# Products with x over 64-row slices, two at a time in the two row halves of TensorE

## The chip, the cores and the metric

The kernel runs on one core of one Trainium2 chip. A core has five engines with queues of their own: TensorE (PE in the profile, with its weight loads in a row of their own, PEld), VectorE (DVE), ScalarE (ACT), GpSimd (POOL) and SyncE (SP), which here only issues DMAs. The metric is the device time of one execution in microseconds. The kernel before takes 1052.12 us, the median of 3 runs (1051.35 to 1052.48). Durations below come from one profiled execution of it, which took 1051.69 us.

## The reference

A gated sum of two branches over the same x, with 2048 tokens of width 448: attention with 16 heads of 28 columns, and a GeGLU feed-forward with 1792 hidden columns. All in fp32.

```python
g = _sigmoid((x * gate_w).sum(-1, keepdims=True))
# a: attention
qkv = (x @ wqkv).reshape(B, S, 3, H, Dh).transpose(2, 0, 3, 1, 4)
q, k, v = qkv[0], qkv[1], qkv[2]
scores = jnp.einsum("bhqd,bhkd->bhqk", q, k) * (Dh ** -0.5)
p = _softmax(scores, axis=-1)
o = jnp.einsum("bhqk,bhkd->bhqd", p, v)
a = o.transpose(0, 2, 1, 3).reshape(B, S, D) @ wo
# b: feed-forward
b = (_gelu(x @ w_gate) * (x @ w_up)) @ w_down
return g * a + (1 - g) * b
```

## The kernel before

**Precision.** An fp32 value is split into a high part, rounded to the type fp32r that TensorE streams fast, and a low part, the rest. A product of two split matrices is three products: high with high, high with low, low with high. ScalarE makes the high parts (`activation(..., Copy)`), VectorE or GpSimd the low ones (`tensor_tensor(..., subtract)`).

**Contracting with x.** x has 448 columns, that is three slices of 128 rows and one of 64. `PAIRS` (L42) lists the products of one output tile: 3 x 3 for the three whole slices, and 2 for the last: there the 64 high rows and the 64 low rows of x stand in one slice of 128 rows, multiplied once with the high and once with the low weights (stored twice, one copy for each half). So 11 products of 128 rows make one tile of 128 columns of weights by 512 tokens. `X` (L65) keeps x for the whole run as 7 slices of 128 partitions by 2048 tokens.

**Stage 1, q and k** (L84 to L193): 28 tiles `pqk` of 11 products each (`qk_tile`, L152), 7 column tiles for each of 4 token blocks. The raw inputs come in on SP and ACT queues, 8 ahead, and `SPLITS` says after which tile each is split: before the first tile stand the first weights and four slices of x. Each tile is split into high and low again and stored to DRAM (`qkd`).

**Stage 2, v and the gate** (`v_tile`, L172): 16 tiles `pv` of 128 tokens by 450 columns, 11 products each. Between them two small groups of products (`pb`, `pr`) bound the scores, so that softmax needs no maximum over rows. A branch (`tc.If`, L251) skips the exact row maxima, as here always. Every engine loads the flag and branches for itself.

**Stage 3, attention** (L285 to L408). For a head, `Q` and `K` hold four copies of 28 rows (high and low in the combinations that the split needs) and two rows for the bound, 114 rows in all, so one product of 128 keys by 512 queries gives finished scores. Heads are loaded one ahead, on the SP queue, into two pairs of buffers. A step is one key tile `kt` and half of the queries: two products into one of three score tiles `sc` (two PSUM banks each), then one `exp` by ScalarE over 128x1024 into `pt` (L307). The products with V (`values`, L310; fp32, four column tiles of 32 side by side into `po`) are done for four key tiles together, three steps after the last of them (`ENDS`, `LATE`): this gives a cycle of 8 steps, and 64 cycles in the run. Products of `x @ w_up` (`pu`, and of the first three tiles of `x @ w_gate`) fill between the steps, two per step (`RATE`), from a generator `up()` through `fill()`; after a finished tile one step goes without, while VectorE copies the one PSUM bank out (`u`, then to DRAM in `ud`).

**Stage 4, feed-forward and output** (L411 to the end). For each pair of hidden tiles: `hidden()` makes 11 products `pg` with w_gate for one token block, GELU on ScalarE, the product with the stored `u`, and the split `hl`; `down()` multiplies with w_down (`pd`, 128x448, 3 products per hidden tile) and adds into `acc` on VectorE. `down` of one block stands behind `hidden` of the next (`pend`). The attention output is multiplied with wo in `project()` in between. The last round writes `y` and sends it out.

**What sets the order.** Products are pinned in program order on TensorE (`mm`, L51, whose second line L52 every product has in the profile). Most of the DMAs, splits and copies are placed by a scheduler when the program is built; each engine then runs its list in order.

Of the kernel before, what the change touches and what calls it, by code (L numbers as in the profile page):

```python
# [17 lines left out]
P = 128  # L18
TB = 512
# [5 lines left out]
FC = 2  # L25
ENDS = (3, 7, 11, 15)
LATE = 3
RATE = 2
NB = 3
ORDER = (2, 3, 1, 4, 0, 5, 6)  # L30
AHEAD = 8
WARM = 9
LAG = 6
NR = 4 * DH + 2
# [3 lines left out]


# [6 lines left out]
def gated_mix(ctx: ExitStack, tc: tile.TileContext, xT, wqk, wvg, wg, wu, wd, wo, sel, ident, out):  # L46
# [13 lines left out]
    ud = dram.tile([NF + NB, P, S], F32, name="ud")  # L60
# [4 lines left out]
    X = keep.tile([P, 7, S], F32R, name="X")  # L65
    fw = ctx.enter_context(tc.tile_pool(name="fw", bufs=2))
    attn = ctx.enter_context(ExitStack())
    vp = attn.enter_context(tc.tile_pool(name="vp", bufs=1))
    V = vp.tile([P, NKT, H, 32], F32, name="V")
    nc.gpsimd.memset(V[:, :, :, DH:], 1.0)  # L70


    halves = {}

    def load_half(src, f, key, hi, mark=lambda ins: ins):
        raw = fw.tile([P, 4, P], F32, name="hraw")
        w = fw.tile([P, 8, P], F32R, name="half", bufs=3)
        mark(nc.sync.dma_start(out=raw, in_=src[f]))
        mark(hi(w[:, 0:4], raw))
        mark(nc.vector.tensor_tensor(w[:, 4:8], raw, w[:, 0:4].bitcast(F32), OP.subtract))  # L80
        halves[key, f] = w


    with ExitStack() as ph:  # L84
        wq = ph.enter_context(tc.tile_pool(name="wq", bufs=1))
        st = ph.enter_context(tc.tile_pool(name="st", bufs=1))
        wp = ph.enter_context(tc.tile_pool(name="wp", bufs=1))
        ps = ph.enter_context(tc.tile_pool(name="ps1", bufs=3, space=PSUM))
        psv = ph.enter_context(tc.tile_pool(name="psv", bufs=2, space=PSUM))
        psb = ph.enter_context(tc.tile_pool(name="psb", bufs=1, space=PSUM))  # L90

        WQK = wq.tile([P, NQK, 8, P], F32R, name="WQK")
        zero = st.tile([P, TB], F32R, name="zero")
        raws = [st.tile([P, TB], F32, name=f"raw{i}") for i in range(AHEAD)]
        WV = wp.tile([P, 8, VW], F32R, name="WV")
        selt = wp.tile([P, NQK, H], F32, name="selt")
        mx = wp.tile([P, NQK, NTB], F32, name="mx")
# [3 lines left out]
        warm = psb.tile([P, TB], F32, name="warm")  # L101
# [5 lines left out]
        SPLITS = {-1: ["w0", "x00", "x01", "x02", "x03"], 0: ["w1", "w2"], 1: ["w3", "x10"],  # L107
# [5 lines left out]

        def load():
            nonlocal issued
            if issued < len(loads):
                a = loads[issued]
                r = raws[issued % AHEAD]
                if a[0] == "w":
# [71 lines left out]
        while stored:  # L191
            store()
# [371 lines left out]
```

## Time and profile before

| | us |
|---|---|
| median of 3 runs | 1052.12 |
| the profiled execution | 1051.69 |
| its span (first to last instruction) | 1049.9 |
| stage 1, to the first `pv` | 77.4 |
| stage 2, to the branch | 37.8 |
| branch to the first scores | 3.9 |
| stage 3, to the last group of `po` | 637.9 |
| that group and the last `pu`, to the first `pg` | 6.2 |
| stage 4 | 286.8 |

A group of instructions stands in one line as `line engine op out<-in rows*columns shape xcount | busy us, mean ns of one | idle before, and what ended it`. A timeline line gives the start, the length from the first to the last of a merged run, the engine and the instructions. A matmul's length is modelled and longer than the distance to the next one, since they are pipelined; so the distance is worked out from runs: (length of the run - mean of one) / (count - 1). Times are us from the start of the span.

### The profile page before, as it was taken

How to read it: one execution, taken by the hardware profiler on the slowest of the kernel's cores; microseconds unless marked ns; L12 is line 12 of the kernel's file. 1: busy time of each engine (PE TensorE's matmuls, PEld its weight loads, DVE VectorE, ACT ScalarE, POOL GpSimd, SP SyncE). 2: the span in 40 equal slices, each digit the busy share in tenths (PEclk: the TensorE clock that was granted, in tenths of full speed). 3: DMA queues.
4: the chain of work that ended last, by engine and by line, in shares of the span. 5: the costliest groups of instructions: out<-in, count | busy, mean ns of one | idle time of the engine just before them, and what ended most of it. 6: DMA issues, size and time to landing. Idle time of an engine off the chain costs nothing.

```text
span 1049.9 us, 14556 instructions
## 1 busy us (share of the span) xinstructions
PE 1041.3 (99%) x5673; PEld 731.4 (70%) x5673; DVE 315.7 (30%) x512; ACT 610.5 (58%) x732; POOL 51.3 (5%) x38
## 2 busy tenths in 40 slices
PE   9999999999999999999999999999999999999998
PEld 6889765655655656656556556556588898899887
DVE  4552112111111011011011111110157666577555
ACT  5332477877777778778777777787643332233321
POOL 4322000000000000000000000000001011100000
PEclk9999999999999999999999999999999999999999
DMA  7865333332332332332332332331264323242223
GB/s 250 306 253 122 79 94 87 118 104 80 108 95 77 111 95 75 108 101 74 104 105 75 98 110 74 96 109 37 70 190 141 112 80 100 88 150 68 67 86 117
DMA packets 58906, 115.84 MB, mean 110 GB/s; under 512 B 12784, under 2 KB 18160, under 8 KB 55216
## 3 DMA queue, kind: packets, MB, share of 16 engines
q1 hardware_dynamic: 58544, 114.32, 36.2%
q8 instruction: 47, 0.77, 0.3%
q10 hardware_dynamic: 288, 0.52, 0.2%
q14 instruction: 27, 0.22, 0.1%
HBM read 74.44 MB, written 40.37 MB: 109 GB/s over the span
## 4 chain that ended last, share of the span: by engine, by line
PE 88%; ACT 0%; issue 0%; DVE 0%; ACTq 0%
PE sc L52 23%; PE po L52 22%; PE pd L52 16%; PE pu L52 16%; PE pg L52 11%; ACT pt L307 0%; DVE y L470 0%; ACT w L431 0%; ACTq L307 0%
## 5 line engine op out<-in xcount | busy, mean ns | idle before, releaser
L307 ACT ACTIVATE pt<-sc 128x1024 f32<-128x1024 f32 x512 | 477.9, 1040 | 160.7 <-PE sc L52 160.4
L52 PE MATMUL sc<-Q,K 128*128 128x512 f32 x1024 | 313.5, 398 | 1.7 <-issue 1.6
L52 PEld LDWEIGHTS sc<-Q,K 128*128 128x128 f32 x1024 | 187.1, 188 | 91.0 <-issue 54.8
L52 PE MATMUL pu<-X,half 128*128 128x512 f32 x748 | 233.3, 391 | 0.1
L52 PE MATMUL po<-pt,V 128*32 128x512 f32 x2048 | 233.0, 595 | 0.0
L352 DVE COPY u<-pu 128x512 f32<-128x512 f32 x68 | 47.0, 691 | 488.3 <-PE pu L52 477.4
L52 PEld LDWEIGHTS pu<-X,half 128*128 128x128 f32 x748 | 140.1, 188 | 32.4 <-issue 1.4
L52 PEld LDWEIGHTS po<-pt,V 128*32 128x32 f32 x2048 | 60.0, 109 | 138.2 <-issue 132.7
L52 PE MATMUL pd<-w,hl 128*128 128x448 f32 x672 | 140.1, 365 | 0.0
L52 PEld LDWEIGHTS pd<-w,hl 128*128 128x128 f32 x672 | 126.2, 188 | 11.1
L52 PE MATMUL pg<-X,half 128*128 128x512 f32 x484 | 114.0, 390 | 0.0
L52 PEld LDWEIGHTS pg<-X,half 128*128 128x128 f32 x484 | 90.9, 188 | 18.4
L52 PE MATMUL pqk<-X,WQK 128*128 128x512 f32 x308 | 70.9, 391 | 1.0 <-ACT X L143 0.8
L52 PEld LDWEIGHTS pqk<-X,WQK 128*128 128x128 f32 x308 | 57.5, 188 | 14.7 <-ACT X L143 1.5
L447 ACT ACTIVATE g<-pg 128x512 f32<-128x512 f32 x44 | 26.2, 594 | 70.3 <-PE pg L52 70.2
L448 DVE TENSOR_TENSOR g<-g,u 128x512 f32<-128x512 f32 x56 | 46.4, 837 | 50.8 <-ACT g L447 50.7
L449 ACT ACTIVATE hl<-g 128x512 fp32r<-128x512 f32 x56 | 35.2, 631 | 42.2 <-DVE g L448 36.8
L467 DVE SCALAR_TENSOR_TENSOR acc<-pd,gate,acc 128x448 f32<-128x448 f32 x80 | 52.7, 679 | 6.0 <-PE pd L52 5.9
L495 POOL TENSOR_TENSOR ohl<-oraw,ohl 128x1536 fp32r<-128x1536 f32 x4 | 14.0, 3502 | 704.8 <-ACT ohl L491 704.8
L450 DVE TENSOR_TENSOR hl<-g,hl 128x512 fp32r<-128x512 f32 x56 | 38.3, 687 | 10.6 <-ACT hl L449 8.5
L162 ACT ACTIVATE hl<-pqk 128x512 fp32r<-128x512 f32 x28 | 16.7, 598 | 41.6 <-PE pqk L52 39.7
L52 PE MATMUL pv<-WV,X 128*128 128x450 f32 x176 | 36.5, 367 | 0.0
(62 smaller groups left out, 357.0 us busy)
## 6 DMA issues: line engine op xcount, KB each, us to landing
ud<-u SPq DMA_DIRECT2D x68, 256.0 KB
qkd<-hl SPq DMA_DIRECT2D x28, 512.0 KB
K<-qkd SPq DMA_DIRECT2D x64, 224.0 KB
Q<-qkd SPq DMA_DIRECT2D x64, 224.0 KB
u<-ud SPq DMA_DIRECT2D x56, 256.0 KB
rb<-rdend SPq DMA_DIRECT2D x64, 64.0 KB
raw<-in_xT SPq DMA_DIRECT2D x14, 256.0 KB
hraw<-in_wu SPq DMA_DIRECT2D x14, 256.0 KB
```

The source lines that it names most:

```text
L52: return pin(nc.tensor.matmul(o, lhsT, rhs, start=start, stop=stop))
L162: pin(nc.scalar.activation(hl[:, 0], p, AF.Copy))
L307: nc.scalar.activation(pt, sc, AF.Exp, scale=SCALE)
L352: nc.vector.tensor_copy(u, p)
L447: nc.scalar.activation(g, pg, AF.Gelu_apprx_tanh)
L448: nc.vector.tensor_tensor(g, g, u, OP.mult)
L449: nc.scalar.activation(hl[:, 0], g, AF.Copy)
L450: nc.vector.tensor_tensor(hl[:, 1], g, hl[:, 0].bitcast(F32), OP.subtract)
L467: nc.vector.scalar_tensor_tensor(acc[:, t], p, g1, acc[:, t], OP.mult, OP.add)
L495: nc.gpsimd.tensor_tensor(O[:, 4:7], o[:, 0:3], O[:, 0:3].bitcast(F32), OP.subtract)
```

## The change

All products that contract over x use slices of 64 rows: 448 is 7 x 64, with no rest. `X` becomes 14 slices (7 high, 7 low): partitions 0 to 63 hold the tokens of the first half (blocks 0 and 1), partitions 64 to 127 those of the second (2 and 3). Weights are stored twice, once in each half of the partitions (`both`). A tile needs 21 products of 64 rows (`UNITS`). They are written alternately for a tile in the lower and one in the upper row half:

```diff
+NS = 7
+HALF = S // 2
-RATE = 2
-NB = 3
+RATE = 4
+NOUT = 68
+UNITS = [(NS * a + s, NS * b + s) for s in range(NS) for a, b in ((0, 0), (0, 1), (1, 0))]
-    X = keep.tile([P, 7, S], F32R, name="X")
+    X = keep.tile([P, 2 * NS, HALF], F32R, name="X")
-        def qk_tile(n):
-            tb, t = divmod(n, NQK)
-            for i, (x, w) in enumerate(pairs):
-                mm(p, WQK[:, t, w, :], X[:, x, s], i == 0, i == len(pairs) - 1)
+        def qk_pair(n):
+            b, t = divmod(n, NQK)
+            p = [ps.tile([P, TB], F32, name="pq") for _ in range(2)]
+            for i, (x, w) in enumerate(UNITS):
+                for g in range(2):
+                    mm(p[g], WQK[side(g), t, w], X[side(g), x, s], i == 0, i == len(UNITS) - 1)
```

`v_pair` does the same for two token tiles of stage 2, and `hidden(f, b)` for the blocks b and b + 2 in stage 4. In stage 1 each load becomes two DMAs of 64 partitions, and nine splits instead of five stand ahead of the first products:

```diff
-        SPLITS = {-1: ["w0", "x00", "x01", "x02", "x03"], 0: ["w1", "w2"], 1: ["w3", "x10"],
+        SPLITS = {-1: ["a0", "x00", "x01", "x02", "x03", "b0", "x04", "x05", "x06"],
+                  **{n: [f"a{n + 1}", f"b{n + 1}", f"x1{n}"] for n in range(6)}, 6: ["x16"],
-            sub = nc.vector if a in loads[:6] else nc.gpsimd
+            sub = nc.vector if done < len(SPLITS[-1]) else nc.gpsimd
```

Scores: `K` holds high and low (56 rows, then rows of ones) in each row half, `Q` has two layers, high and low, each twice in each row half, so 512 queries of scores are two products of 64 rows into one bank. Q takes 8 DMAs per head instead of 4, K 4 as before, and the bound 2 instead of 1. In a step the four products of the scores stand in one row half and up to four products of one `x @ w_up` tile in the other; `run` deals them out alternately. Two steps of a cycle get no units: the one with the values, and the one behind it.

```diff
+        def run(todo):
+            while todo[0] or todo[1]:
+                g = min((g for g in range(2) if todo[g]), key=lambda g: free[g])
+                todo[g].pop(0)()
+                free[g] = max(free[g], free[1 - g] - 1) + 1
-        def scores(h, kt, half):
+        def scores(h, kt, half, n):
+            n = min(n, left())
+            if n:
+                f = block["g"]
+                todo[f] += [unit] * n
+                to = (1 - f, 1 - f if n > 1 else f)
+            else:
+                f = min(range(2), key=lambda g: free[g])
+                to = f, 1 - f
             for c in range(2):
-                mm(sc[:, c * 512:(c + 1) * 512], K[:, kt * P:(kt + 1) * P],
-                   Q[:, half * 1024 + c * 512:half * 1024 + (c + 1) * 512], True, True)
+                g = to[c]
+                for a in range(2):
+                    todo[g].append(lambda g=g, a=a, c=c: mm(
+                        sc[:, c * 512:(c + 1) * 512], K[side(g), kt * P:(kt + 1) * P],
+                        Q[side(g), a, half * 1024 + c * 512:half * 1024 + (c + 1) * 512], a == 0, a == 1))
+            run(todo)
-        fill(11)
+        two_blocks()
-                    spaced(h, kt, half)
                     count += 1
+                    spaced(h, kt, half, 0 if due and count == LATE or count == LATE + 1 and h + kt > 3 else RATE)
```

`two_blocks` computes two tiles side by side in a score tile's two banks; one call stands ahead of the first scores, one ahead of the last values. In stage 4 the four `hidden` calls of a pair of hidden tiles now stand together ahead of its four `down` calls; the pool `gp` of w_down's split tiles is made only there (before, it was set aside ahead of attention); the output tile takes the two buffers of `gs` where `y` had three:

```diff
-                    y = tp.tile([P, TB], F32, name="y")[:, 0:D]
+                    y = tp.tile([P, TB], F32, name="gs", bufs=2)[:, 0:D]
+            for b in range(2):
+                for i, f in enumerate(chunk):
+                    if b == 0 and n * FC + i + 1 < NF:
+                        load_f(ORDER[n * FC + i + 1])
+                    for tb, hl in zip((b, b + 2), hidden(f, b)):
+                        hls.setdefault(tb, []).append(hl)
+            for i, tb in enumerate((0, 2, 1, 3)):
+                down(n, tb, hls[tb])
```

Three places of the built order follow. On PE, one cycle of attention in the middle of the run, from one group of values to the next. Before (sc are scores, pu products of `x @ w_up`, po values; the middle repeats):

```order
L52 MATMUL po<-pt,V 32x512 x16
L52 MATMUL sc<-Q_956,K_957 128x512 x2
L52 MATMUL pu<-X,half 128x512 x2
...
L52 MATMUL pu<-X,half 128x512
L52 MATMUL sc<-Q_956,K_957 128x512 x4
L52 MATMUL po<-pt,V 32x512 x16
```

That is 16 sc and 11 pu in a cycle. After, each product a half of the rows:

```order
L60 MATMUL po<-pt,V 32x512 x16
L60 MATMUL sc<-Q_1441,K_1442 128x512 x4
L60 MATMUL pu<-X,half 128x512
L60 MATMUL sc<-Q_1441,K_1442 128x512
...
L60 MATMUL pu<-X,half 128x512
L60 MATMUL sc<-Q_1441,K_1442 128x512 x8
L60 MATMUL po<-pt,V 32x512 x16
```

Now 32 sc and 21 pu stand in a cycle, pu and sc in turn for the most part, with 4 sc alone behind the values and 8 nearly alone ahead of them.

On PE, around the branch (gsc products stand in the branch that is not taken). Before:

```order
L250 TENSOR_LOAD flag
L52 MATMUL pu<-X,half 128x512 x2
L251 COMPARE_AND_BRANCH
...
L251 UNCONDITIONAL_BRANCH x2
L52 MATMUL pu<-X,half 128x512 x9
L52 MATMUL sc<-Q_956,K_957 128x512 x4
```

After:

```order
L60 MATMUL pq<-WV,X 128x450 x84
L294 TENSOR_LOAD flag
L295 COMPARE_AND_BRANCH
...
L295 UNCONDITIONAL_BRANCH x2
L60 MATMUL sc<-X,half 128x512 x42
L60 MATMUL pu<-X,half 128x512
```

The 11 pu around the branch needed only their own PSUM bank. The 42 products of `two_blocks` that now stand first write banks 0 and 1, which the last `v_pair` used, so their first waits for ScalarE's and VectorE's copies of those. On POOL the fills of Q's and K's constant rows, which stood ahead of the branch, now stand behind it but for one, and so do 11 of head 0's 12 loads on SP.

On ACT, the start of stage 4. Before:

```order
L447 ACT_TABLE_LOAD
L447 ACTIVATE g<-pg 128x512 x2
L449 ACTIVATE hl_8061<-g 128x512
L449 ACTIVATE hl_8091<-g 128x512
L447 ACTIVATE g<-pg 128x512
```

After:

```order
L553 ACTIVATE g<-gs 128x512 x2
L327 ACTIVATE half<-hraw 128x896
L555 ACTIVATE hl_10382<-g 128x512
L555 ACTIVATE hl_10388<-g 128x512
L527 ACTIVATE w<-draw 128x448 x2
L553 ACTIVATE g<-pg 128x512 x2
L553 ACTIVATE g<-gs 128x512
L527 ACTIVATE w<-draw 128x448
L555 ACTIVATE hl_10447<-g 128x512
```

The first GELUs of products (`g<-pg`) and the split of their result (`hl_10447`) now stand behind three splits of w_down (`w<-draw`), whose loads share one buffer `draw`; before, w_down's first tiles were loaded and split during attention.

More of the change, by code (lines that the diff above doesn't have):

```diff
@@ L358, in gated_mix, with unit, two_blocks, spaced @@
+        def unit():
+            nonlocal hold
+            product(block)
+            if block["n"] == len(UNITS):
+                hold = 3
+        def two_blocks():
+            sc = psc.tile([P, 1024], F32, name="sc")
+            todo = []
+            for g in range(2):
+                start(sc[:, g * 512:(g + 1) * 512])
+                b = dict(block)
+                todo.append([lambda b=b: product(b)] * len(UNITS))
+            block["n"] = len(UNITS)
+            run(todo)
         hold = 0
-        def fill(n):
+        def spaced(h, kt, half, n):
@@ L405, in gated_mix @@
         hold = 0
[L406 to L407 removed]
+        while left():
+            unit()
+            hold = 0
     attn.close()
```

367 lines of the change are left out of this document (199 added, 168 removed), and 3 rows, old and new, of the table SPLITS.

## The prediction

> **What bounds the kernel now.** I read the page's busy times first, then its chain, then the stages.
>
> ```profile
> span 1049.9 us, 14556 instructions
> PE 1041.3 (99%) x5673; PEld 731.4 (70%) x5673; DVE 315.7 (30%) x512; ACT 610.5 (58%) x732; POOL 51.3 (5%) x38
> PE sc L52 23%; PE po L52 22%; PE pd L52 16%; PE pu L52 16%; PE pg L52 11%; ACT pt L307 0%; DVE y L470 0%; ACT w L431 0%; ACTq L307 0%
> PEclk9999999999999999999999999999999999999999
> ```
>
> TensorE is busy for the whole span at full granted clock, and the chain runs through its products from end to end. So the time is the number of products by the distance between them, and what TensorE waits. By stages (us, then busy us of PE, PEld, DVE, ACT, POOL, then clock, DMA share, GB/s):
>
> ```profile
> 6.50:77.40 70.90, 70.71 (x309) 57.66 (x310) 38.19 (x60) 29.20 (x52) 26.24 (x21) 1.00 0.77 274
> 77.40:115.20 37.80, 37.67 (x207) 34.02 (x206) 8.27 (x31) 9.32 (x17) 7.06 (x4) 1.00 0.40 99
> 119.10:757.00 637.90, 637.81 (x3766) 382.22 (x3766) 86.63 (x149) 480.14 (x518) 0.00 (x0) 1.00 0.32 93
> 763.20:1050.00 286.80, 282.38 (x1333) 249.93 (x1332) 180.03 (x268) 89.45 (x142) 16.84 (x8) 1.00 0.37 110
> ```
>
> DMA is below 0.4 except in stage 1. ACT is next: 480 of 638 us in attention, nearly all of it in the exps. The distances come from long runs:
>
> ```profile
> 763.26 10.14 PE L52 MATMUL pg<-X,half 128*128 128x512 f32 x44
> 87.30 27.31 PE L52 MATMUL pv<-WV,X 128*128 128x450 f32 x132
> 1035.69 9.89 PE L52 MATMUL pd<-w,hl 128*128 128x448 f32 x48
> L52 PE MATMUL pg<-X,half 128*128 128x512 f32 x484 | 114.0, 390 | 0.0
> L52 PE MATMUL pqk<-X,WQK 128*128 128x512 f32 x308 | 70.9, 391 | 1.0 <-ACT X L143 0.8
> L52 PE MATMUL pu<-X,half 128*128 128x512 f32 x748 | 233.3, 391 | 0.1
> L52 PE MATMUL pv<-WV,X 128*128 128x450 f32 x176 | 36.5, 367 | 0.0
> ```
>
> (10.14 - 0.39) / 43 gives 0.227 us for a product of 512 columns, (27.31 - 0.37) / 131 gives 0.206 for 450, and (9.89 - 0.37) / 47 gives 0.203 for 448.
>
> **What a pair costs.** The change replaces 11 products by 21 of half the rows, two at a time, or 10.5 pairs. All hangs on T, the distance between pairs of 512 columns, which no row shows. The only rows with several products at once are those of the values, whose four column tiles run together:
>
> ```profile
> 428.43 0.13 PEld L52 LDWEIGHTS po<-pt,V 128*32 128x32 f32 x4 [0.30 <-issue]
> 428.85 0.13 PEld L52 LDWEIGHTS po<-pt,V 128*32 128x32 f32 x4 [0.30 <-issue]
> 429.28 0.13 PEld L52 LDWEIGHTS po<-pt,V 128*32 128x32 f32 x4 [0.30 <-issue]
> 429.71 0.13 PEld L52 LDWEIGHTS po<-pt,V 128*32 128x32 f32 x4 [0.30 <-issue]
> 431.54 0.30 PEld L52 LDWEIGHTS sc<-Q,K 128*128 128x128 f32 x2 [0.84 <-issue]
> ```
>
> Each round of four starts 0.428 after the one before (1.28 / 3). If a round streams its 512 columns at half the rate of the others, its half is 0.214: 0.013 less than 0.227, so that in tiles little is lost between products. Lower end: pd and pg differ by 64 columns and 0.024 us; 512 columns at that slope are 0.192. Upper ends: 0.227, if a half loses between products what the whole array does, and more if weight loads get in the way. Two loads of 128 columns with no product between start 0.11 apart (0.30 less one load of 0.188, the last row), so two loads in turn need 0.22. I take **T = 0.217**, near the row of the tiles.
>
> The page "TensorE: Matmul & The Clock Gate" of the Trainium skill (Part 3, "What overlaps and what doesn't") says that weight loads overlap products under way only where row groups differ. The trace disagrees for the whole array: the loads' mean of 0.188 lies inside a distance of 0.227 in which a product of the same rows streams.
>
> **Stage 1.** 308 x 0.227 = 69.9 of its 70.9 us become 294 x 0.217 = 63.8. The start gets longer: nine splits stand ahead of the first pair, on DVE at 0.69 each, and the next weights are split on POOL:
>
> ```profile
> 7.38 2.02 DVE L146 TENSOR_TENSOR X<-raw,X 128x512 fp32r<-128x512 f32 x3 [0.17 <-ACT X L143]
> 13.96 1.29 POOL L146 TENSOR_TENSOR WQK<-raw,WQK 128x512 fp32r<-128x512 f32 x1
> ```
>
> From 5.9 us, where the first split starts, nine take DVE to about 12, 0.6 later than 21 T from 6.5 would be; then the second pair's low weights want a POOL split of 1.3 behind loads that reuse buffers: 1.9 lost in all, where 1.0 was. 63.8 + 1.9 - 70.9 = **-5.2**.
>
> **Stage 2.** 168 pairs of 450 columns for 176 products. Between 0.188 (0.206 less the 0.013, and less what the lower slope gives) and 0.22 (two loads in turn) I take 0.200: 33.6 - 36.2 = **-2.6**.
>
> **The branch.** The last products of stage 2 end at 114.4.
>
> ```profile
> 114.64 0.54 ACT L176 ACTIVATE V<-pv 128x448 f32<-128x448 f32 x1 [1.71 <-PE pv L52]
> 115.22 0.16 DVE L177 COPY gate<-pv 128x1 f32<-128x1 f32 x1 [2.10 <-ACT V L176]
> 115.22 2.29 PE L52 MATMUL pu<-X,half 128*128 128x512 f32 x9
> 119.12 1.16 PE L52 MATMUL sc<-Q,K 128*128 128x512 f32 x4 [1.62 <-issue]
> 119.39 0.69 DVE L352 COPY u<-pu 128x512 f32<-128x512 f32 x1 [4.02 <-DVEq L251]
> ```
>
> Scores wait until VectorE, behind its last copy, has loaded the flag and branched (4.02 us idle). In these 4.7 us 11 pu ran (2.5). Now nothing runs, since the first pair of tiles waits for VectorE too, and the wait ends a V copy of 0.54 later: 5.2 - 4.7 = **+0.5**, with the pair of tiles counted below. POOL's fills and head 0's loads, now behind the branch on their queues, are covered: both engines pass their branch as soon as the flag is there, some 15 us before TensorE, and the pair of tiles adds 21 T = 4.6; each us that they were later than that would cost one, once. The same page (Part 1) says that an idle gap of over about 3.4 us halves TensorE's clock for about as long; no stretch after the start here is that long. By it the sum would be 1.7 higher, an estimate.
>
> **Attention.** A cycle is 437.97 - 428.04 = 9.93 us:
>
> ```profile
> 428.04 3.57 PE po L52 x32
> 437.05 0.92 PE sc L52 x4
> 437.97 3.57 PE po L52 x32
> 441.54 0.66 PE sc L52 x2
> 432.37 7.45 ACT L307 ACTIVATE pt<-sc 128x1024 f32<-128x1024 f32 x8 [2.48 <-PE sc L52]
> L307 ACT ACTIVATE pt<-sc 128x1024 f32<-128x1024 f32 x512 | 477.9, 1040 | 160.7 <-PE sc L52 160.4
> ```
>
> The values keep 3.57. The other 6.36 hold 16 + 11 products: 27 x 0.227 = 6.13, and 0.23 for changing between whole rows and column tiles (0.66 for the two sc behind the values instead of 0.45). Now there are 32 + 21 halves, 53, or 27 pairs with the odd one: 27 x 0.217 + 0.23 + 3.57 = 9.66. The exps set a second limit. Eight lie (7.45 - 1.04) / 7 = 0.916 apart; the first starts 432.37 - 428.04 = 4.33 behind the values' start. The eighth step needs the score tile of the fifth exp, since there are three: 4.33 + 4 x 0.916 + 1.04 = 9.03. Then its scores (2 T = 0.43) and the change to the values (0.15): 9.61. So both limits meet, and a T under 0.215 brings nothing more here. 9.66 - 9.93 is -0.27, for 62 cycles -16.7. Outside them stand, by the same rows, 27.9 us now (from 119.12 to 763.26, less 62 cycles), and then two pairs of tiles (9.1), the first steps (9.1), a last cycle (8.8) and values (3.6): 30.6. Together **-14.0**. Q's additional DMAs (16 x 4 x 0.224 MB in 638 us, 23 GB/s on 93) and SP's longer list lie beside; a head is loaded some 39 us ahead, so they cost nothing until the list takes that long.
>
> **Stage 4.** 484 x 0.227 = 109.9 become 462 x 0.217 = 100.3: -9.6. Pairs and whole products alternate seven times, at 0.33 (0.23 and about 0.1 within the 3.57): +2.3. The first pd starts 42 T = 9.1 us in; its second operand stands on ACT behind three loads of w_down through one buffer (each about 2.5 to land, 0.6 and 0.7 to split): ready at about 11.5, +2.4. The output has two buffers:
>
> ```profile
> L470 DVE SCALAR_TENSOR_TENSOR y<-pd,gate,acc x16: 677/684/684, 1017.4 to 1045.6; 128x448 f32<-128x448 f32 x16
>   DMA out<-y: 1.1, 1
> ```
>
> Three buffers held a tile every 6 x 0.203 = 1.22 with one wait of 1.1, that is in 3.65 us or less; two would give at most 1.8 a tile and at least 1.22, so 0 to 9 over 16 tiles. With 0.7 to compute and about 2 to land it is 1.36: +2.0. Sum **-2.9**.
>
> **The sum.** -5.2 - 2.6 + 0.5 - 14.0 - 2.9 = -24.2. From the profiled 1051.69 this is 1027.5; the median shown stands 0.4 higher, so **1028**. Each 0.001 of T is worth 0.29 (stage 1) + 0.17 + 1.7 (62 x 27) + 0.46, or about 2.6 us above 0.217.
>
> **Rivals.**
> - *A half is no quicker than the whole.* T between 0.222 and 0.229: at 0.227, 1028 + 26 = 1054; 1041 to 1059. For it: nothing in a row says which part of the 0.227 is lost between products, and each half is a small array with the same loads. Against: the rounds of the values. 0.20.
> - *Weight loads take turns* (the slow side). Two loads per pair where one was. At 0.11 each they fit; from T = 0.2265 the change loses, which takes loads 0.003 longer each. At 0.12 each, T = 0.240: 1028 + 60 = 1088. For it: PEld is already 88% busy in stage 4. Against: the values' loads start together, four in 0.13. 0.15.
> - *A half's load waits for its own product*, the rule weighed above: T = 0.217 + 0.188 = 0.405, and 1028 + 490 = 1518. The loads of the whole array speak against it. 0.02. That the halves don't run together at all would be slower still and is in this chance.
> - *The small losses don't come* (start, w_down, output): 6 less, and with T = 0.2145 another 4: 1018, or 1012 with the slope's 0.192 in stages 1, 2 and 4. 0.03 below 1012.
>
> **How the numbers follow.** The forecast, T from 0.2145 to 0.221, has 0.60 and runs from 1014 to 1040. A measurement here tells about 0.2% from no change, that is 1050 to 1054. Faster: 0.60 + 0.03 + 0.09 (the rival with T under 0.2255); same 0.06; slower 0.22. The range 1012 to 1060 takes in the forecast and the first rival and leaves out 0.20: the two slow ones and the far low end.
>
> **What would show it.** Runs of pq in stage 1: 42 products in 21 T, 4.6 us a pair of tiles (4.8 if halves are no quicker, 5 if loads take turns). Values 9.6 to 9.7 apart, with TensorE waiting for exps just ahead of the last scores of a cycle if T is at its lower end, and no wait at 0.22. About 5 us without products at the branch; a wait at the first pd; the last outputs about 1.36 apart. The forecast is wrong if T lies above 0.222, or if scores wait at the start of each head.

## The result: slower, and the profile after

The changed kernel takes 1083.02 us, the median of 4 runs (1081.29 to 1085.46), beside 1052.3 for the kernel before: a ratio of 1.0295, 95% interval 1.0273 to 1.0318. The forecast was 1028, the range ended at 1060. The page of the changed kernel, a profiled execution of 1081.29 us:

```profile
span 1079.5 us, 20134 instructions
...
PE 1047.9 (97%) x8257; PEld 733.0 (68%) x8257; DVE 332.9 (31%) x515; ACT 612.3 (57%) x740; POOL 69.2 (6%) x47
...
PEclk9999899999999999999999999999998999999999
```

TensorE was busy for 1041 us before and is busy for 1048 now, though every tile takes 10.5 pairs where it took 11 products. And 32 us are idle, where it was 9. By stages, from the starts of the first and last products in the two traces, beside the terms of the forecast (the starts of stages as in the table of before):

| us | before | after | difference | forecast |
|---|---|---|---|---|
| to the first v product | 77.4 | 77.8 | +0.4 | -5.2 |
| v, to the last product's start | 36.8 | 35.0 | -1.9 | -2.6 |
| then to the first product behind the branch's wait (before, 11 `pu` ran within it) | 4.9 | 6.5 | +1.6 | +0.5 |
| then to the first `pg` | 644.1 | 657.0 | +12.8 | -14.0 |
| to the last product | 282.0 | 296.2 | +14.3 | with the end: -2.9 |
| to the end | 4.7 | 7.1 | +2.4 | |
| span | 1049.9 | 1079.5 | +29.6 | -24.2 |

**Pairs.** The timeline of a cycle of attention (start, length, engine, instruction):

```profile
405.68 3.64 PE L60 MATMUL po<-pt,V 128*32 128x512 f32 x32
...
412.09 0.39 PE L60 MATMUL sc<-Q,K 64*128 64x512 f32 x1
412.10 0.39 PE L60 MATMUL pu<-X,half 64*128 64x512 f32 x1
...
414.36 0.39 PE L60 MATMUL sc<-Q,K 64*128 64x512 f32 x1
414.37 0.39 PE L60 MATMUL pu<-X,half 64*128 64x512 f32 x1
...
415.61 3.64 PE L60 MATMUL po<-pt,V 128*32 128x512 f32 x32
```

A score and a `pu` start together, so the halves do run side by side. But from 412.09 to 414.36 ten pairs pass: 0.227 each, what a whole product took. Values to values is 9.93 us, to the hundredth what it was: 27 pairs for 27 products. In stage 1 the pairs of tiles stand 4.76 us apart (25.40 to 30.16), the 4.8 that the prediction named for a half no quicker than the whole.

**Waits and the clock.** What TensorE waited for, and the windows around its longest gaps (us, then busy us of PE, PEld, DVE, ACT, POOL, then granted clock, that is the share of its full clock that TensorE was given, then DMA share and GB/s):

```profile
PE sc L60 <- DVEq L295: 6.1, 1, 6.1
PE pd L60 <- DVE acc L575: 5.0, 3, 4.5
PE sc L60 <- DVE u L429: 3.7, 2, 2.9
PE pd L60 <- DVE acc L573: 3.6, 3, 2.0
PE pq L60 <- ACT X L161: 2.5, 1, 2.5
```

```profile
8.20:12.70 4.50, 4.40 (x24) 3.24 (x26) 4.09 (x8) 3.25 (x6) 0.00 (x0) 0.64 0.80 225
...
112.90:119.10 6.20, 0.18 (x2) 0.00 (x0) 0.32 (x2) 0.98 (x2) 2.79 (x1) 0.69 0.62 136
119.10:122.30 3.20, 3.12 (x16) 2.72 (x18) 0.00 (x0) 0.00 (x0) 0.00 (x0) 0.53 0.01 3
...
767.10:770.30 3.20, 0.31 (x4) 0.01 (x1) 1.99 (x3) 1.23 (x2) 0.00 (x0) 1.00 0.70 216
770.30:774.10 3.80, 3.80 (x18) 1.08 (x22) 1.78 (x2) 0.95 (x1) 0.00 (x0) 0.55 0.85 266
...
826.50:831.10 4.60, 0.15 (x1) 0.00 (x0) 3.23 (x6) 3.20 (x7) 0.00 (x0) 0.74 0.68 232
831.10:835.40 4.30, 4.29 (x12) 3.81 (x13) 4.30 (x8) 2.08 (x5) 0.00 (x0) 0.50 0.76 242
```

After each gap of over 3 us (start to start 3.17 at the first products, 6.47 at the branch, 3.27 at the end of attention, 4.83 in stage 4) the granted clock is about half for the next 3 to 4 us, and the products then stand 0.37 to 0.42 apart. "Busy" counts that as work. The gap of 2.36 us at 806 has no such sequel.

### The profile page after: what moved, and what is told of

Same layout as the page of the kernel before. It is cut to its first block, busy times and chain, and to the rows that moved or that the text cites. A ratio compares the mean times of both kernels' runs of the same rounds, so it can differ in the third digit from the quotient of the medians.

```text
span 1079.5 us, 20134 instructions
## 1 busy us (share of the span) xinstructions
PE 1047.9 (97%) x8257; PEld 733.0 (68%) x8257; DVE 332.9 (31%) x515; ACT 612.3 (57%) x740; POOL 69.2 (6%) x47
## 4 chain that ended last, share of the span: by engine, by line
PE 77%; DMA 4%; ACT 3%; DVE 3%; issue 2%; SPq 0%; DVEq 0%; ACTq 0%
PE po L60 21%; PE sc L60 21%; PE pu L60 16%; PE pd L60 11%; PE pg L60 8%; ACT pt L378 2%; DMA out<-gs 1%; DMA u<-ud 1%; DVE ohl L601 1%; DMA oraw<-in_wo 1%; DVE gs L578 1%; DMA oraw<-od 1%; DMA draw<-in_wd 1%; DVE g L554 0%; DMA gs<-ud 0%
## 5 line engine op out<-in xcount | busy, mean ns | idle before, releaser
L378 ACT ACTIVATE pt<-sc 128x1024 f32<-128x1024 f32 x512 | 477.7, 1041 | 170.6 <-PE sc L60 169.5
L60 PE MATMUL sc<-Q,K 64*128 64x512 f32 x2048 | 413.8, 399 | 0.6 <-ACT pt L378 0.4
L60 PEld LDWEIGHTS sc<-Q,K 64*128 64x128 f32 x2048 | 314.5, 184 | 83.3 <-issue 50.3
L60 PE MATMUL pu<-X,half 64*128 64x512 f32 x1344 | 317.4, 387 | 0.0
L60 PEld LDWEIGHTS pu<-X,half 64*128 64x128 f32 x1344 | 247.1, 184 | 33.9 <-issue 1.7
L60 PE MATMUL pg<-X,half 64*128 64x512 f32 x924 | 106.9, 388 | 0.0
L60 PEld LDWEIGHTS pg<-X,half 64*128 64x128 f32 x924 | 88.1, 184 | 18.5 <-issue 2.7
L60 PE MATMUL pq<-X,WQK 64*128 64x512 f32 x588 | 69.2, 394 | 3.1 <-ACT X L161 2.5
L60 PEld LDWEIGHTS pq<-X,WQK 64*128 64x128 f32 x588 | 56.1, 188 | 16.4 <-ACT X L161 3.3
L555 ACT ACTIVATE hl<-g 128x512 fp32r<-128x512 f32 x56 | 33.9, 629 | 24.8 <-DVE g L554 20.6
L554 DVE TENSOR_TENSOR g<-g,u 128x512 f32<-128x512 f32 x56 | 36.7, 687 | 33.3 <-ACT g L553 28.5
L60 PE MATMUL pd<-WO,ohl 128*128 128x448 f32 x176 | 36.7, 367 | 0.0
```

The costliest lines, as they stand in the source:

```text
L60: return pin(nc.tensor.matmul(o, lhsT, rhs, start=start, stop=stop))
L378: nc.scalar.activation(pt, sc, AF.Exp, scale=SCALE)
L554: nc.vector.tensor_tensor(g, g, u, OP.mult)
L555: nc.scalar.activation(hl[:, 0], g, AF.Copy)
```

## The experiments

Ratios are to the kernel before on the same chip. A difference of a few us between two variants of the changed kernel says little: its own four runs differ by 4 us, where those of the kernel before differ by 1.3. Every position in a trace comes from one profiled execution.

### What a pair costs

**e1.** Products of zeros ahead of stage 1, in twelve series (one run):

```diff
+        def series(count, rows, wide, cols):
+            for i in range(count):
+                r = rows[i % len(rows)]
+                mm(bank[r.start // 64][0:wide, 0:cols], zero[r, 0:wide], zero[r, 0:cols], True, True)
+        series(40, [whole], P, 512)
+        series(24, [lower], P, 512)
+        series(48, [lower, upper], P, 512)
...
```

> The changed kernel with extra products of zeros ahead of stage 1 (their time is added, their result is not used): series of whole products (128 rows), of products in the lower 64 rows alone, and of lower and upper in turn, each with 512, 448 and 256 columns, and with 128, 64 or 32 columns of weights. Theory A (a fixed loss of about 0.013 us with each change of weights, in each row half as in the whole array): the distance of a pair equals that of a whole product at every width, 0.2265 at 512, 0.203 at 448 and about 0.12 at 256, and a product in the lower half alone has the same distance. Theory B (a half could be as quick as 0.214, but the two loads of weights of a pair hold it up): the lower half alone is quicker than the whole, below 0.22, and only the pairs stand at 0.2265; at 256 columns the pairs fall behind the whole, to 0.2 or more. If the loss belongs to the width of the loaded weights, 32 columns of weights give 0.214 to 0.216 at 512.

Windows inside the series (us, busy us and count of PE, clock, DMA share, GB/s), in the order whole, lower half alone, pairs, first with 512 columns, then with 256:

```profile
8.00:14.00 6.00, 6.00 (x28) 1.00 0.80 218
16.50:19.50 3.00, 3.00 (x15) 1.00 0.70 178
22.00:25.00 3.00, 3.00 (x29) 1.00 0.50 136
...
41.00:43.40 2.40, 2.40 (x22) 1.00 0.00 0
44.00:46.00 2.00, 2.00 (x19) 1.00 0.00 0
47.00:49.20 2.20, 2.20 (x41) 1.00 0.00 0
```

A window holds, beside its own, one or two records that began ahead of it. The lower half alone is as slow as the whole, and of the pairs about as many halves pass in 3 us as whole products in 6: two halves in the time of one whole. The distances from start to start in one lane:

| columns | whole | lower half alone | each half of a pair |
|---|---|---|---|
| 512 | 0.227 | 0.227 | 0.226 to 0.240 |
| 448 | 0.203 | 0.202 | 0.205 |
| 256 | 0.120 | 0.120 | 0.120 |

Theory A holds, and B falls: the lower half alone is no quicker. From 256 to 512 columns the distance grows by 0.1066, or 0.000416 us a column; by that line 512 columns take 0.213, and 0.0135 is lost with each product, whatever its rows and whether another runs beside it. (448 columns lie 0.003 above the line, so the split of the 0.2265 is rough; that halves and wholes agree is not.) The guess that the loss belongs to the width of the weights failed: with 32 columns of weights the distance is 0.232, not 0.214. Whether it belongs to the change of weights or to the product itself is open, since every product here loads its own.

### The branch, the clock and the end of attention

**e2** put products of zeros into two gaps (15 instead of 9 at the start, 24 behind stage 2):

```diff
-WARM = 9
+WARM = 15
+        dummy = psb.tile([P, TB], F32, name="pb")
+        for _ in range(24):
+            mm(dummy, zero[:, 0:P], zero, True, True)
```

> The changed kernel with products of zeros in two of its idle gaps: 15 instead of 9 at the start, and 24 behind the last product of stage 2. They end before the waits do, so the work itself starts no earlier. Theory (a gap of about 3 us lets the granted clock fall to half for some 4 us): the products behind the two gaps run at 0.2265 from the first on instead of 0.42, which saves 2.3 us at the start and 1.5 us at the branch, 3.8 in all. Rival (the slow products come from what else runs there, loads, splits or the branch itself): nothing is saved, and the products stay at 0.42.

1096.6 us, ratio 1.0424 (1.0407 to 1.0442). The clock did as the theory said, 1.00 behind both:

```profile
7.86:12.70 4.84, 4.30 (x30) 2.65 (x30) 3.72 (x7) 3.04 (x6) 0.00 (x0) 1.00 0.65 189
...
119.10:125.60 6.50, 5.43 (x43) 4.24 (x41) 0.68 (x1) 0.00 (x0) 6.01 (x3) 1.00 0.00 1
```

But nothing was saved. At the start v still began at 78.5 (77.8 without): the products, now quick, waited for the splits. In this run the ninth split ended 0.9 us later than in the changed kernel (15.0, where it was 14.1) and the third pair of tiles started 0.7 later (21.4, 20.6), so the half clock cost little there: the splits were later than it. At the branch the zeros lie in memory that Q and K take over, so POOL's fills started at 119.6 instead of 96.2, head 0's loads behind them, and the first scores waited 12.3 us more. That is the price of the fills when their cover is gone.

**e9** repeated the second half with products of x, which hold up no fill:

> The changed kernel with 24 products of x with itself (their result is not used) behind the last product of stage 2. Unlike the earlier products of zeros they hold no memory that the fills of Q and K wait for. Theory (the idle gap at the branch lets the granted clock fall to half): the granted clock behind the wait is 1.00 instead of 0.53, the 42 products of the first pair of tiles take 4.8 us instead of 6.0 without the gap for the copy, and head 0 is in time. Rival (the first products behind the branch are slow for the branch's sake): they stay at 0.39 to 0.42 for some 3 us.

Here the wait at the branch lasted to 123.5, 5.0 us beyond the last of the 24, and the clock fell again (1089.5 us, one run). So it doesn't tell the theory from its rival; e2 does, by the clock of 1.00 at both places.

**e3** moves the copies of a pair of tiles behind its last product, which wrote into the other half of the tile being copied:

```diff
-                todo.append([lambda b=b: product(b)] * len(UNITS))
+                todo.append([lambda b=b: product(b, False)] * len(UNITS))
             run(todo)
+            for b in bs:
+                copy_out(b)
```

> The changed kernel, but in a pair of tiles of the scores' banks the copies of both stand behind the 42nd product instead of one ahead of it. Theory (the 42nd product waits for the copy out of the other half of its tile, and at the end of attention this wait also drops the clock): the gap of 1.2 us ahead of the first scores goes, and at the end of attention the gap of 3.3 and the four rounds of values at 0.83 go: 1.0 + 3.0 + 1.6 = 5.6 us less. Rival (something else is late there, such as the stores or the exps): the wait stays and moves to the next instruction, under 1.5 us less.

1083.6 us, 1.0315 (1.0294 to 1.0335), so no gain, and yet both gaps went: first scores at 125.8 instead of 126.8, first `pg` at 770.3 instead of 776.2, 5.9 us where 5.6 were expected. Stage 4 gave them back: 301.9 us instead of 296.2, with 4.2 between starts ahead of its fourth pd. Its loads came only 2 to 3 us earlier (the first of w_down was issued at 771.9 instead of 775.2, wo's at 795.6 instead of 797.9).

**e4** computes the first pair of tiles in the banks of `po` and `pu`:

```diff
-        two_blocks()
+        two_blocks([pso.tile([P, TB], F32, name="po"), psu.tile([P, TB], F32, name="pu")])
```

> The changed kernel, but the first pair of tiles at the branch goes into the banks of po and of pu, which nothing of stage 2 holds late, instead of a score tile. Theory (the pair waits only for VectorE to copy the last tiles of stage 2 and to pass its branch): the 42 products run from 113 on while VectorE is in its branch, at full clock, and the first scores start at about 120.5 instead of 126.8: 6 us less. Rival (TensorE itself passes the branch late, or head 0's loads or POOL's fills are not there by 120): the first scores wait for those, and under 3 us is saved.

1078.4 us, 1.0264 (1.0247 to 1.0281): 4.6 less. The 42 products run from 113.3 at full clock, and the first scores start at 122.5; ahead of them stand 3.55 us between two starts, since the next `pu` needs the bank whose copy stands behind VectorE's branch. That is short of the 6 us of the theory, and over the 3 of the rival.

**e16** asks why that branch takes so long, by loads beside it in the kernel before:

```diff
     load_q(heads[0][0], 0)
+    for _ in range(4):
+        load_k(heads[1][1], 1)
+        load_q(heads[1][0], 1)
```

> The kernel before, with head 1's Q and K loaded four times more ahead of the branch (the same values again), so that DMAs run while VectorE passes the branch. Theory (VectorE's code behind the branch comes in slower beside other traffic): its idle time at the branch rises from 4.0 to 6 or more. Rival (it depends on where the code lies, or on what VectorE runs ahead): it stays at 3.8 to 4.5.

The window of its branch, and the timeline line of VectorE's first copy behind it:

```profile
114.00:119.00 5.00, 2.81 (x13) 2.00 (x11) 0.85 (x2) 0.55 (x1) 0.00 (x0) 1.00 0.89 188
```

```profile
116.90 0.69 DVE L355 COPY u<-pu 128x512 f32<-128x512 f32 x1 [1.82 <-PEq L254]
```

With DMA at 0.89 VectorE was through in 1.82 us, quicker than the 4.02 of before. The theory falls, and the rival's 3.8 to 4.5 isn't met either. (The first scores then waited for SP behind its loads, 1077.0 us in one run.) What sets the branch's length stays open: TensorE's wait for it was 6.1 us in the changed kernel and 8.4 in e5, which has the same instructions there.

### Stage 4

**e5**, **e6** and **e7** change one thing each: three buffers for w_down's loads; wo's and the attention output's splits behind pd's additions; three output buffers.

```diff
-            draw = gp.tile([P, TB], F32, name="draw")[:, 0:D]
+            draw = gp.tile([P, TB], F32, name="draw", bufs=3)[:, 0:D]
```

> The changed kernel with three buffers for the loads of w_down instead of one. Theory (in the first 20 us of stage 4 ScalarE and VectorE stand behind three loads of w_down that follow one another through one buffer, and the first pd with them): the gaps of 0.6, 0.7 and 1.65 us at 786 to 793 go, 2.4 us less, and nothing after 800 changes. Rival (the loads of u, of the ready x @ w_gate tiles and the last head's stores, on the same SP queue, set the start): the gaps stay within 1 us, and the time with them.

```diff
-                load_wo()
+                with tc.issue_after(last.ins):
+                    load_wo()
...
-                    load_o((n - 1) * 2 + i // 2)
+                    with tc.issue_after(last.ins):
+                        load_o((n - 1) * 2 + i // 2)
```

> The changed kernel, but the splits of wo and of the attention output are put on VectorE behind the additions of the tiles of pd before them (and so behind the GELU products of their round) instead of ahead of them. Theory (VectorE waits in order for the load of wo, and then for that of the output, while pd waits for VectorE to empty its banks): the gaps of 2.4 us at 806 and of 4.8 at 826 go, and the half clock that follows the second: 2.1 + 4.6 + 1.9 = 8.6 us less. Rival (it is the load of u that is late, whatever stands on VectorE): the gap at 826 stays at over 3, and at most 2.5 us is saved.

```diff
-                    y = tp.tile([P, TB], F32, name="gs", bufs=2)[:, 0:D]
+                    y = tp.tile([P, TB], F32, name="y", bufs=3)[:, 0:D]
```

> The changed kernel with three output buffers of their own, as before the change, instead of two shared ones. Theory (with two buffers each tile of the last round waits for the store two ahead of it): the small gaps among the last 12 pd (0.17, 0.24 and 0.25) go, and the end comes 4.7 us behind the last product instead of 7.1: 3.1 us less. Rival (the stores land late for another reason): the end stays 7 us behind, under 1 us less.

None gained: 1088.5 (1.0355, 1.0335 to 1.0374), 1083.2 (1.0301, 1.0284 to 1.0319), 1085.2 (1.0314, 1.0297 to 1.0331). In e5 gaps of 2.6 and 3.3 stand where 0.7 and 1.65 stood, which neither its theory nor its rival has. In e6 the gap of 2.4 at 806 is gone and the one of 4.8 is still there (4.0 and 1.1): its rival. In e7 the end is as its theory has it, 4.35 behind the last product instead of 7.11, and stage 4 is 7.4 longer.

What that wait of 4.8 in the changed kernel hangs on is shown by the chain of work that ends in it (some of its pieces: start, length, what), and by two lines of the timeline:

```profile
808.75 5.70 DMA oraw<-od
814.47 0.64 ACT ohl L600
...
819.86 1.64 DVE g L554 x3
821.49 5.59 DMA u<-ud
827.18 0.70 DVE g L554
...
831.11 4.91 PE pd L60 x13
```

```profile
815.13 4.07 DVE L601 TENSOR_TENSOR ohl<-oraw,ohl 64x512 fp32r<-64x512 f32 x1 [2.78 <-ACT ohl L600]
815.16 3.49 POOL L602 TENSOR_TENSOR ohl<-oraw,ohl 128x1536 fp32r<-128x1536 f32 x1
```

The attention output lands, is split, VectorE goes on, past a split of w_down, to three products `g`, these free the buffers of `u`, the next `u` is loaded in 5.6 us, and only then can VectorE reach the additions that empty pd's banks. In between VectorE is held up: its split of 64x512 takes 4.07 us beside GpSimd's split of 128x1536, as all four do in this kernel (3.37 to 4.07), where the first of them in e17 stands clear of it and takes 0.69. In e17 a product `g` beside that split takes 3.59 instead of 0.69. The kernel before has the same (a `g` of 3.67 at 787.1), with no wait of TensorE behind it. No run moved GpSimd's split, so what it costs here is not shown.

**e8** and **e10** put the edits together (e10 with wo's splits later on ScalarE too, and five buffers for `u`):

> The changed kernel with the edits of the earlier runs together: copies of a pair of tiles behind its 42nd product, the first pair in the banks of po and pu (and no further products of x @ w_up in the first three steps), three buffers for w_down's loads, wo and the attention output split later, three output buffers (shared with the ready gate tiles). Theory (what is left over the rival with a pair at 0.2265 are these waits): 6 + 6 + 2 + 8 + 3 = 25 us less than the changed kernel, about 1058, still not below the kernel before, since a pair is no quicker than a whole product. Rival (the loads and stores around the start of stage 4 are a limit of their own, and a wait that goes comes back behind it): over 1066.

> The edits of e8, with one buffer for w_down's loads again, five instead of three for the loads of u, and the splits of wo and of the attention output behind their round's GELU work on ScalarE too, not only on VectorE. Theory (stage 4 waits for loads that stand in order ahead of GELU work, last the attention output's on ScalarE, 8 us idle): the gap of 4.8 + 1.1 us at 815 in e8 goes with its half clock, about 7 us less than e8, 1064. Rival (the first round's loads and w_down's splits are the limit, and later waits only follow): within 2 us of e8's 1071.6.

1071.6 (1.0189, 1.0172 to 1.0206) and 1069.3 (1.017, 1.0153 to 1.0187). e8's rival holds; e10 is 2.3 us below e8, close to its rival (2) and not to its theory (7). What is won lies ahead of stage 4 (first `pg` at 767.9 and 765.1) and at the end; stage 4 itself stays at 297.3 and 297.2.

**e11** lets the products with w_down follow one pair of blocks behind, as before the change; **e12** is that with the edits of e3 and e4:

```diff
-            for i, tb in enumerate((0, 2, 1, 3)):
...
-                down(n, tb, hls[tb])
+                for a in pend:
+                    down(*a)
+                pend = [(n, tb, hls[tb]) for tb in (b, b + 2)]
```

> The changed kernel, but in stage 4 the products with w_down follow one pair of blocks behind the GELU work, as they did one block behind before the change (four buffers for w_down's split tiles, three for the outputs, shared). Theory (the waits come from the order: two pairs of tiles of pg, then at once the pd that need their GELU results and splits): waits of pd above 0.6 us fall from 11.2 us in all to under 4, the half clock goes with them, seven more changes between pairs and whole products cost 2: stage 4 from the first pg to the last product 296.2 to about 286, and the time 1073. Rival (the loads at the start of stage 4 are a limit whatever the order): stage 4 stays over 292.

> e11 and the edits at the branch and in the pairs of tiles (copies behind the 42nd product; first pair in the banks of po and pu). Theory: e11 less the 10 us that e3's earlier end of attention and e4 gave, about 1062; not below the kernel before, which a pair at 0.2265 could beat by at most the half product saved per tile. Rival: what is won ahead of stage 4 is lost in its waits, over 1068.

1090.9 (1.0371, 1.0354 to 1.0389) and 1082.2 (1.0293, 1.0275 to 1.031): worse than without the edit, stage 4 at 303.9 and 310.4, beyond the bounds of both rivals.

**e13**, **e14** and **e15** turn it round and put the change's two other edits of stage 4 into the kernel before, apart and together: w_down's pool made only in stage 4; all GELU tiles of a round ahead of its pd (with eight buffers for their results, as the change has, where four were).

> The kernel before, with the pool of w_down's split tiles made in stage 4 instead of ahead of attention, so that its first loads and splits come only there; products and order as before. Theory (the loads of stage 4, no longer hidden by attention, are most of its loss): waits of pd appear in the first 60 us and the time rises by 3 to 8 us. Rival (down stands one block behind hidden and covers the loads; the loss is in the change's order): within 1 us of before.

> The kernel before, with w_down's pool as before, but in stage 4 all eight GELU tiles of a round ahead of its four groups of pd, wo and the attention output loaded one round earlier as in the change, and the outputs in three shared buffers. Theory of the loads: under 3 us slower. Rival (the order: in-order ScalarE and VectorE stand behind wo's and the output's loads while pd waits): 6 to 12 us slower, with gaps of over 2 us at the round that loads wo and the output.

> The edits of e13 and e14 together in the kernel before. If the two are what stage 4 of the changed kernel lost, and pairs have no part in it, stage 4 from the first pg to the last product gets 16 to 20 us longer than its 282.0 (the change: +14.3 with 3.9 us saved by its 22 fewer pairs); if pairs have a part (their changes to whole products, a slower pd), under 12.

1051.5 (1.0005, 0.9995 to 1.0014), 1055.0 (1.0037, 1.0023 to 1.005) and 1053.2 (1.0019, 1.0009 to 1.0029). e13's rival holds, and e14's 3.7 us lie between its two forecasts. With whole products neither edit makes a wait of pd (e14 and e15 have one wait of a `pg`, 1.5 and 1.4 from start to start); stage 4 of e15 takes 283.4 us, 1.4 more than before where 16 to 20 would have put the loss on the two edits. So neither w_down's late loads nor the new order is the loss by itself, and by e15's terms pairs have a part in it; which part, these runs don't tell.

**e17** undoes the change's third edit there, how the tiles are dealt to rounds; **e18** is e10 with it:

```diff
-ORDER = (0, 4, 1, 5, 2, 6, 3, 7, 8, 9, 10, 11, 12, 13)
+ORDER = (4, 5, 6, 7, 2, 3, 8, 9, 0, 1, 10, 11, 12, 13)
```

> The changed kernel with the hidden tiles paired into rounds as before the change: (4, 5), (6, 7), (2, 3), (8, 9), (0, 1) and so on, instead of (0, 4), (1, 5), (2, 6) and so on. Only the order changes. Theory (each of the first rounds has 9.5 us of products for 8 tiles' loads, GELUs and splits, and with 19 us the loads are covered as they are in e15): waits of pd above 0.6 us fall from 11.2 us to under 3, the half clock in stage 4 goes, and stage 4 takes 283 to 286 us instead of 296.2: 1071 to 1074. Rival (the pairs themselves hold stage 4 up, through the 64-row loads of weights or the doubled splits): it stays over 292, and the time over 1078.

> e10 with the rounds as in e17. Theory: first pg at 765 as in e10, stage 4 283 to 286, 4.4 behind it: a span of 1053 to 1056, a time of 1055 to 1058, within 0.6% of the kernel before and not below it, since a pair at 0.2265 saves half a product per tile and the changes between pairs and whole products, the start and the branch take that back. Rival: over 1064.

1086.7 (1.033, 1.0314 to 1.0346) and 1069.9 (1.0175, 1.0158 to 1.0192): rivals again. But e17 gathers the waits into one, of 15.4 us, and shows their kind. TensorE's wait, and ScalarE's list around it:

```profile
PE pd L60 <- DVE acc L573: 15.4, 1, 15.4
```

```profile
792.69 0.63 ACT L555 ACTIVATE hl<-g 128x512 fp32r<-128x512 f32 x1 [0.31 <-DVE g L554]
801.00 1.70 ACT L588 ACTIVATE WO<-oraw 128x1792 fp32r<-128x1792 f32 x1 [7.67 <-DMA oraw<-in_wo]
802.60 0.58 ACT L553 ACTIVATE g<-pg 128x512 f32<-128x512 f32 x1
```

The same place in e15, whole products:

```profile
784.47 0.63 ACT L449 ACTIVATE hl<-g 128x512 fp32r<-128x512 f32 x1 [0.24 <-DVE g L448]
790.88 1.70 ACT L480 ACTIVATE WO<-oraw 128x1792 fp32r<-128x1792 f32 x1 [5.77 <-DMA oraw<-in_wo]
```

In both ScalarE waits some 6 to 8 us for wo to land, and wo isn't later in e17: its split starts 25.7 us behind the first `pg`, 27.8 in the changed kernel and 28.0 in e15. In e15 all GELUs of the round are done by then, and nothing of TensorE's stands behind. In e17 GELUs of the same round stand behind it, so VectorE's products, the first pd's additions and the banks of pd wait too, through wo's split and the load of the attention output behind it. In e18, where wo is put later, another load has the same place:

```profile
798.36 0.95 ACT L327 ACTIVATE half<-hraw 128x896 fp32r<-128x896 f32 x1 [7.97 <-DMA hraw<-in_wg]
```

The waits ahead of pd, taken from all distances over 0.6 us between starts, less 0.203 each, and summed over stage 4: none in the kernel before, e13, e14 and e15; 11.2 us in the changed kernel, 9.0 to 19.4 in its variants (9.0 in e2, 10.3 in e6, 13.5 in e10, 17.3 in e17, 19.4 in e12). No variant beats the kernel before; e10, the best, is 1.7% behind.

## Why the prediction was wrong

**The step that failed first is T.** The prediction took the 0.013 us between 0.214 and 0.227 for a loss of the whole array that halves would not have, from the rounds of the values, where four column tiles run at once and 512 columns at half rate take 0.428. e1 shows the loss in each row half, paired or alone. Column tiles of fp32 were the wrong row to go by: it said that several products run at once, and nothing of what a half loses between two. By the forecast's own counts, T at 0.2265 (and 0.208 in stage 2, 34.95 us by 168) takes back 2.8 + 1.3 + 17.1 + 4.4 = 25.6 of the 53.8 us between -24.2 and +29.6. With it alone the time would be 1053, its first rival. That rival had 0.20; the forecast's 0.60 was too much for a value that no row showed.

**The other 28 us are waits**, with products at half clock and some slower cycles. They come on top of the some 6 (0.9 + 0.5 + 2.4 + 2.0) that the prediction gave to waits.

- *Start*: nine splits were to cost 0.9 more than before; stage 1 is 4.7 us beyond 294 x 0.2265, 2.8 more than forecast. The mechanism, splits that hold up the first pairs, was right. The term mis-sized is when the splits end: the first product came at 8.2 instead of 6.5, and the ninth split ended at 14.1 instead of about 12, because ScalarE waited for each of the last three slices of x to land (0.50, 0.36 and 0.46 us).
- *Branch*: the wait of the first pair for VectorE was right in kind, 6.5 us instead of 5.2. The half clock behind it was set aside ("no stretch after the start here is that long"), though the prediction's own 5.2 us without products is longer than the limit that it cites. It came: 0.53 in the 3.2 us behind the wait, and 1.00 there in e2, which has no such gap. The page "TensorE: Matmul & The Clock Gate" of the Trainium skill (Part 1) gives about 3.4 us of idle as the limit. In the changed kernel 3.17 us from start to start were enough, and 2.36 were not. But the length alone doesn't settle it between 2.4 and 2.8: half clock followed 2.40 in e2 (up to 824.1) and 2.45 at the start of e7 (up to 7.2), and didn't follow 2.49 in e4 (up to 806.5) and 2.76 in e12 (up to 790.1).
- *Within attention*: 9.8 us beyond the pairs. About 2.8 in the first pair of tiles (half clock, and the 42nd product's wait for a copy from the same tile), 4.7 at the end by the same wait and its half clock (e3 removes both and gains 4.9 there), 2.1 over the 62 cycles, nine of which take 10.1 to 10.4 instead of 9.93; what these nine wait for is open. The wait for the copy wasn't foreseen: the prediction put it at nothing. The limit of the exps (9.61) never set a cycle; scores waited 0.4 us for exps in all.
- *Stage 4*: the prediction expected a first wait for w_down (+2.4), seven changes of mode (+2.3) and the outputs (+2.0). All three came about as priced: the waits ahead of the first pd are 2.9 us (in four pieces), pairs to whole products and back cost about 0.4 each time (forecast 0.33), and the outputs, two buffers, came 1.39 us apart (forecast 1.36), worth 2.8 in e7. But the waits are 11.2 us in all, and their half clock some 2 more. The step that failed is that it looked for one late operand at the start and put all waits behind it at nothing: 8.3 us of waits came there. What holds TensorE in e17 are splits that wait for a load and stand in ScalarE's and VectorE's lists ahead of GELU work of the same round, and in the changed kernel the chain through the attention output and `u`. e6, e10 and e18 each put a split later, and another wait stays or shows up.

That head 0's loads and the fills would be covered was right, and Q's doubled loads cost nothing. Why the paired kernel's lists are put in that order, and why pairs and not whole products suffer from it, isn't settled. The change loads each weight in four DMAs instead of one and has fewer buffers for them (two and one for `half` and `hraw`, where three and two were), and its loads start behind the copies of attention's last pair of tiles; that these make loads late is not shown, and for wo it isn't so (25.7 to 28.0 us behind the first `pg`, latest in e15, where nothing waits for it). GpSimd's hold on VectorE is untested too. Also open: why pd with w_down is 0.206 us now in most rounds, where it was 0.203 (about 2 us in all).

## What to carry to other kernels

Splitting the contraction over two row halves could win here what it saves in half-filled slices and no more (10.5 pairs for 11 products; stage 2 won its 1.9 us so): each half has its own loss between products, and a pair the distance of a whole product. A price that no row shows is worth a series of zeros before the rewrite. And where TensorE is at 99%, look first at what stands in order ahead of the work that feeds it, since a gap of 3 us was paid again in half clock, and what was won ahead of such a wait came back in it (e3).

## What the runs showed of the hardware

- A product of 512 columns stands 0.2265 us from the next, at 128 rows, at 64 rows alone and for each of two halves side by side (0.226 to 0.240). With 32 columns of weights it is no less (0.232). By the distances at 256 and 512 columns about 0.0135 of it doesn't go with the columns (e1).
- In these traces every distance of 3.1 us or more between two starts at full clock was followed by half clock for 3 us or more (3.0 behind the branch in the changed kernel, 5.7 behind the 15.8 in e17); of those between 2.4 and 2.8, some were (2.40 in e2) and some not (2.76 in e12). Where the other engines are later than the slow products, it costs little (e2's start).
- The same branch took VectorE, from its last copy to its first release, 1.8 us (e16), 4.0 (before), 4.9 (changed kernel), 7.2 (e5) and 9.1 (e9). DMA traffic with a share of 0.89 didn't lengthen it (e16, one run).
- VectorE operations that take 0.69 us by themselves took 3.4 to 4.1 beside a split of 128x1536 on GpSimd (changed kernel, L601).
